# Loading q and k of the first two batches by token range, and moving block 1's attention work to later places

## The chip, the cores and the metric

The kernel runs on one core of a Trainium2 chip. A core has a matrix engine (TensorE, PE in the profile, with its weight loads as PEld), a vector engine (VectorE, DVE), an activation engine (ScalarE, ACT), a general engine (GpSimd, POOL) and a queue engine (SyncE, SP); sixteen DMA engines move data between device memory and the on-chip SBUF. Matrix products land in PSUM banks. Each engine works through its own list of instructions in order, and semaphores tie the lists together. The metric is the device time of one execution in microseconds (us).

## The reference

Eight batches of attention in chunks of 64 tokens are followed by a gated two-layer product over all 4608 tokens.

```python
# q, k, v: (8 batches, 8 heads, 576 tokens, 64), cut into 9 chunks of 64
scores = scale * q_c @ k_c.T            # per chunk, 64 x 64
attn = softmax(scores)
x = (attn @ v_c) -> (8*576 tokens, 8*64)
h = x @ w_in                            # 512 -> 2048
g = h * sigmoid(beta * h)
out = g @ w_out                         # 2048 -> 512, float32
```

## The kernel before, in words

The 4608 tokens are worked on in nine blocks of 512 (`BLK`). A batch has 576 tokens, so a block and a batch do not coincide: block 0 is tokens 0 to 511 of batch 0; block 1 is tokens 512 to 575 of batch 0 and 0 to 447 of batch 1. A group `g` of scores is four chunks (256 tokens), two groups to a block; a tile `i` of PV is 128 tokens, four to a block.

For one block the work is: scores (`emit_sc`, L156), exponentials on ScalarE (L178), the product with v and a column of ones (`emit_pv`, L212), division by the sum on VectorE (`normed`, L190 and L191), a transpose of the 128-token tile into `xt`, by TensorE and a ScalarE copy (`emit_xp`, L232, L238) or by a DMA transpose (L222), then L1 (16 products `m` with w_in, each followed by a Silu on ScalarE: `emit_h` L259, `emit_g` L270) and L2 (products with w_out). `emit_m(j, m, pieces)` writes one `m` of L1 in `pieces` column ranges. Block 0 has its own entrance: `head_sc`, `head_pv`, `head_xp` and `L1_first`, which work by halves of the heads (`z`) so that they can begin before all heads are there. Blocks from 1 on use a seven-product scheme (Strassen-Winograd) for L2 (`steps_L2`, with sums of `gt` by `emit_sum` and differences of w_out by `emit_tw`), blocks from 2 on also for part of L1. L2 of block 0 (`L2_plain(0)`) is plain: twenty units, for t = 0 to 3 in turn, over w_out rows 0-3, 4-7, 8-11, 12-13 and 14-15; the first twelve units hold four products each and the last eight two each. It holds all four PSUM banks of pool `ps_p`, one per t, and its result is copied by ScalarE (even t, L535) or VectorE (odd t, L533).

w_out is divided by beta row group by row group (`scale_w_out`): most on VectorE (L126), some on ScalarE (L122, the argument `act`). q and k arrive as [32 t-lines x 4 heads, run of tokens, 64] and are brought into [64 dims, tokens] form by 32x32 block transposes on VectorE (`emit_T`, L135), one for q and one for k per half of the heads.

Order is written by hand (`manual_schedule`): every engine does its instructions as the program lists them. All loads that convert float32 to float16 are issued by GpSimd into one queue: q and k of batch 0 (four loads), v of batch 0 (four), w_in (five), w_out 0-1 and 2-3 (a pair number covers 256 rows), q and k of batch 1 (four), w_out 4-5, v of batch 1 (four), w_out 6, w_out 7, q and k of batch 2, and so on. The eight load semaphores are used in turn, so GpSimd issues a load only after the one eight places ahead has landed. The buffers for raw q and k are two deep (`qk`), so batch 3 writes where batch 1 was; transposed q and k are three deep (`qt`); `ps_s` (tags sc0, sc1) and `ps_x` (tag x) hold one buffer each.

Inside `L2_plain(0)` the dictionary `hooks` puts block 1's attention between the units: scores of groups 2 and 3 ahead of unit 8, PV of tiles 4 to 7 ahead of units 11, 12, 14, 16, the tile transposes ahead of 12, 14, 16, 18, and the scalings of w_out rows 12 to 15 ahead of 11 and 14. `L1_plain(1, ...)` follows, with its own hooks for VectorE's later transposes and w_out differences.

Of the kernel before, what the change touches and what calls it, by code (L numbers as in the profile page):

```python
# [15 lines left out]
def kernel(  # L16
# [10 lines left out]
    nc = tc.nc  # L27
# [9 lines left out]
    BLK = 512  # L37
    NB = NT // BLK
    HM = DM // 2
    VP = 80  # L40
    scale = 1.0 / float(D) ** 0.5

# [38 lines left out]
    q_t = {}  # L81
    k_t = {}

    def load_qk(b, split=False):
        for dst, nm in ((q_t, "qu"), (k_t, "ku")):
            dst[b] = qk_p.tile([128, 2, RUN, D], FP16, tag=nm, name=nm)
        for zs in ((slice(0, 1), slice(1, 2)) if split else (slice(0, 2),)):
            for src, dst in ((q, q_t), (k, k_t)):
                nc.gpsimd.dma_start(
                    out=dst[b][:, zs].rearrange("p z r d -> p z (r d)"),  # L90
                    in_=src[b].rearrange("(z a) (t r) d -> (a t) z (r d)", z=2, r=RUN)[:, zs],
                )

    def load_v(b, zs=(0, 1)):
        t = vbuf[b % NV]
        for z in zs:
            for hp in range(2):
                h0 = 4 * z + 2 * hp
                nc.gpsimd.dma_start(  # L99
                    out=t[64 * hp:64 * hp + 64, 2 * z:2 * z + 2, :, 0:D].rearrange(  # L100
                        "p s c d -> p (s c) d"),
                    in_=v[b, h0:h0 + 2].rearrange("s (c p) d -> p (s c) d", p=CH),
                )
# [8 lines left out]
    def load_w_out(m0, n=2):  # L112
        nc.gpsimd.dma_start(
            out=w_out16[:, m0:m0 + n].rearrange("p m r d -> p m (r d)"),
            in_=moe_w_out[m0 * 256:(m0 + n) * 256, :].rearrange(
                "(m p r) d -> p m (r d)", p=128, r=2),
        )
# [10 lines left out]
    qT = {}  # L128
    kT = {}

    def emit_T(b, z, which):
        src, dst, nm = ((q_t, qT, "qT"), (k_t, kT, "kT"))[which]
        if b not in dst:
            dst[b] = qt_p.tile([128, 2, 32, RUN, 2], FP16, tag=nm, name=nm)
        nc.vector.transpose(  # L135
            out=dst[b][:, z].rearrange("p t r e -> p (t r e)").bitcast(FP32).rearrange(
                "p (t r) -> p r t", r=RUN),
            in_=src[b][:, z].rearrange("p r d -> p (r d)").bitcast(FP32).rearrange(
                "p (r d) -> p r d", r=RUN),
        )  # L140

    def T_items(b):
        return [lambda z=z, w=w: emit_T(b, z, w) for z in range(2) for w in range(2)]

    et_t = {}
    sc_h = {}
# [1 line left out]
    def sc_part(g, z, sc):  # L148
        for c in range(4):
            b, cb = divmod(4 * g + c, NCB)  # L150
            for e in range(2):
                for a in range(4):
                    p0, o0 = 32 * a, 64 * (a // 2)
                    kk = kT[b][p0:p0 + 32, z].rearrange("p t r e -> p (t r) e")
                    qq = qT[b][p0:p0 + 32, z].rearrange("p t r e -> p (t r) e")
                    nc.tensor.matmul(  # L156
                        out=sc[a % 2][o0:o0 + 64, z, c, :],
                        lhsT=kk[:, cb * CH:(cb + 1) * CH, e],
                        rhs=qq[:, cb * CH:(cb + 1) * CH, e],
                        start=(e == 0),  # L160
                        stop=(e == 1),
                    )
# [436 lines left out]
    def L1_first():  # L599
        gt_t[0] = gt_p.tile([128, KFF, BLK], FP16, tag="gt", name="gt")  # L600

        def part(g, z):
            for m in range(4):
                emit_h(0, m, g * 256, (g + 1) * 256, (z, 2 + z))
                if (g, z) == (1, 1):
                    emit_g(0, m)

        part(0, 0)
        head_xp(0, 1, "x")
        table(ACTF.Silu)  # L610
        part(1, 0)
        head_xp(1, 1, "s1", eng=nc.vector)
        part(0, 1)
        part(1, 1)
        for m in range(4, 6):
            hps_t[0, m] = ps_s.tile([128, BLK], FP32, tag=f"sc{m % 2}", name="hps")
        for m in range(4, KFF):
            emit_m(0, m, 4 if m < 12 else 1)

    def L1_plain(j, hooks, pieces={}):  # L620
        gt_t[j] = gt_p.tile([128, KFF, BLK], FP16, tag="gt", name="gt")
        for m in range(KFF):
            hooks.get(m, lambda: None)()
            emit_m(j, m, pieces.get(m, 1))
            if m == 8:
                for p in (0, 2):
                    emit_sum(j, 3, p)
        for p in range(4):
            fill.extend([lambda w=w, p=p: emit_sum(j, w, p) for w in (1, 2)])
        hooks.get(KFF, lambda: None)()  # L630
# [24 lines left out]
        nc.scalar.activation(out=warm2, in_=warm, func=func, scale=1.0)  # L655

    with tc.manual_schedule():
        load_qk(0, split=True)
        nc.vector.memset(zero, 0.0)
        nc.vector.memset(bstage, 0.0)  # L660
        nc.vector.memset(warm, 0.0)
# [13 lines left out]
            load_w_in(g)  # L675
        load_w_out(0)
        load_w_out(2)
        load_qk(1, split=True)
        load_w_out(4)
        load_v(1)  # L680
        load_w_out(6, 1)
        load_w_out(7, 1)
        load_qk(2)

        d = emit_idle(88, w=8)
        emit_idle(11, d=d)
        for f in T_items(0):
            f()
        nc.vector.transpose(
            out=bt, in_=bstage.rearrange("p r i -> p (r i)").rearrange("p (i r) -> p r i", r=2)  # L690
# [23 lines left out]
        emit_sw()  # L714
        scale_w_out(range(0, 4))
        scale_w_out(range(4, 8))
        for f in T_items(1):
            f()
        scale_w_out(range(8, 12), act=2)
        emit_tw(1)  # L720
        table(ACTF.Exp)
        load_v(2)
        load_qk(3)
        hooks = {
            8: lambda: [emit_sc(2, "x"), emit_sc(3)],
            11: lambda: [emit_pv(4, xbar=False), scale_w_out((12, 13), act=1)],
            12: lambda: [emit_pv(5, xbar=False), emit_xp(4)],
            14: lambda: [scale_w_out((14, 15), act=1), emit_pv(6, xbar=False), emit_xp(5)],
            16: lambda: [emit_pv(7, xbar=False), emit_xp(6)],
            18: lambda: [emit_xp(7), table(ACTF.Silu)],  # L730
        }
        for kk, f in enumerate(L2_plain(0)):
            hooks.get(kk, lambda: None)()
# [17 lines left out]
        for j in range(1, NB):  # L751
            na = j + 1
            late = j == 1
            if late:
                L1_plain(1, {
                    3: lambda: emit_tw(3), 4: lambda: T(2), 5: lambda: T(2),
                    6: lambda: emit_tw(2), 7: lambda: T(2), 9: lambda: T(2),
                    10: lambda: emit_tw(4), 14: lambda: T(3), 15: lambda: T(3),
                    11: lambda: [loads(1), loads_v(1)],
                    KFF: lambda: [table(ACTF.Exp), emit_sc(4, "x"), emit_sc(5)],  # L760
                }, pieces={0: 4, 1: 4, 2: 4, 3: 4, 4: 4, 5: 2})
            else:
                L1(j, {8: lambda: loads(j), 10: lambda: T(j + 2), 11: lambda: loads_v(j),
                       13: lambda: T(j + 2), 14: lambda: T(j + 2) if j + 2 < B else [dve(2), emit_sum(j, 3, 0)],
                       15: lambda: [dve(2), emit_sum(j, 3, 2)] if j + 2 >= B else None})

            def pv(n, where):
                if na < NB:
                    emit_pv(4 * na + n, where)

            mm, cB, cD, cC = steps_L2(j, last=(j == NB - 1))
            def pvs(n):
                pv(n, "x")
                pv(n + 1, "s")
# [74 lines left out]
```

The softmax here doesn't subtract the row's maximum and nothing guards it: scores larger than these inputs give would overflow.

## Time and profile before

| | |
|---|---|
| median of 3 executions | 276.07 us (276.04 to 276.81) |
| profiled execution, own time | 276.81 us |
| its span in the profile | 275.0 us |
| TensorE busy | 266.9 us (97%) |
| VectorE busy | 214.9 us (78%) |
| ScalarE busy | 164.3 us (60%) |
| GpSimd busy | 96.8 us (35%) |
| granted TensorE clock | full in all 40 slices |
| queue of converting loads (q0) | 18.35 MB, 45024 packets |
| queue of stores and DMA transposes (q1) | 12.99 MB, 24448 packets |

The profile is one execution. "Busy" adds up the time of an engine's instructions; the chain of work that ended last follows the execution back from its last instruction, at each step to what released it. In lists of instructions the columns are start, duration, engine, line, operation, output and input, and in brackets the time that the engine stood idle ahead of it and what ended the wait. The difference between an execution's own time and its span lies outside the engines' instructions. The ends of TensorE products are modelled, so two groups that follow each other closely can overlap in the list.

### The profile page before, as it was taken

What the parts mean: (1) busy time and instruction counts of PE and PEld (TensorE: products, weight loads), DVE (VectorE), ACT (ScalarE), POOL (GpSimd) and SP (SyncE); (2) the same over time, 40 slices, a digit from 0 to 9 for tenths busy, and PEclk for the clock granted to TensorE, in tenths of its full rate; (3) what the DMA queues carried; (4) which work ended last, traced back from release to release, by engine and by line L of the source; (5) the groups of instructions that cost most, each with busy time, mean ns of one, the idle gap of its engine ahead of it and who ended that gap; (6) DMA issues with size and microseconds to landing.
All of it is one profiled execution on the core that took longest, in us unless ns stands there. A gap on an engine that the chain in (4) does not pass through costs nothing.

```text
span 275.0 us, 8686 instructions
## 1 busy us (share of the span) xinstructions
PE 266.9 (97%) x3751; PEld 197.1 (72%) x3751; DVE 214.9 (78%) x429; ACT 164.3 (60%) x281; POOL 96.8 (35%) x107
## 2 busy tenths in 40 slices
PE   8699999999999999999999999999999999999994
PEld 5379544857886688768876886688668866886784
DVE  2673674877888999799989988997689768986844
ACT  2169527879166845784578447854784478316820
POOL 8643446171108720772077205720311031112110
PEclk9999999999999999999999999999999999999999
DMA  6999999999967934893479242924202320232013
GB/s 103 171 200 210 210 181 208 194 261 199 90 135 144 172 44 117 173 163 42 117 158 173 45 120 76 87 42 117 79 0 60 100 76 0 55 104 76 0 42 114
DMA packets 69654, 32.02 MB, mean 116 GB/s; under 512 B 53744, under 2 KB 63984, under 8 KB 69616
## 3 DMA queue, kind: packets, MB, share of 16 engines
q0 software_dynamic: 45024, 18.35, 55.3%
q1 hardware_dynamic: 24448, 12.99, 18.1%
q8 instruction: 29, 0.48, 0.7%
q10 hardware_dynamic: 144, 0.13, 0.1%
q14 instruction: 9, 0.07, 0.1%
HBM read 36.71 MB, written 9.44 MB: 168 GB/s over the span
## 4 chain that ended last, share of the span: by engine, by line
PE 79%; DMA 14%; DVE 3%; issue 1%; ACT 1%; POOL 1%; DVEq 0%; ACTq 0%; POOLq 0%
PE hps L259 22%; PE oA L416 19%; PE wA L313 9%; PE wX L313 7%; DMA w_out<-in_moe_w_out_dram 6%; PE oB L416 5%; PE oD L416 5%; DMA wi<-in_moe_w_in_dram 4%; PE oC L416 4%; DMA ku<-in_k_dram 3%; PE ops L518 2%; PE x L212 2%; DMA xt<-x 1%; PE scx L156 1%; PE sc L156 1%
## 5 line engine op out<-in xcount | busy, mean ns | idle before, releaser
L259 PE MATMUL hps<-xt,wi 128*128 128x512 f16 (+2 forms) x528 | 85.2, 308 | 0.2
L270 ACT ACTIVATE gt<-hps,beta 128x512 f16<-128x512 f32 x88 | 57.8, 683 | 20.9 <-PE hps L259 20.7
L259 PEld LDWEIGHTS <-wi 128*128 128x128 f16 x528 | 42.8, 98 | 23.2 <-DMA wi<-in_moe_w_in_dram 0.2
L416 PEld LDWEIGHTS <-s 128*128 128x128 f16 x496 | 47.6, 98 | 6.2 <-DVE s L376 0.5
L416 PE MATMUL oA<-tw,s 128*128 128x256 f16 x368 | 44.2, 273 | 0.0
L416 PEld LDWEIGHTS <-gt 128*128 128x128 f16 x384 | 36.3, 98 | 6.6
L427 ACT COPY u<-oA 128x512 f32<-128x512 f32 x24 | 14.0, 585 | 40.3 <-PE oA L416 40.3
L321 DVE COPY u<-wA 128x512 f32<-128x512 f32 x42 | 28.6, 682 | 4.5 <-PE wA L313 4.5
L99 POOL DMA_DIRECT2D vb<-in_v_dram x32 | 27.4, 873 | 6.3 <-DMA w_out<-in_moe_w_out_dram 3.3
L344 POOL TENSOR_TENSOR t<-u,w 128x512 f32<-128x512 f32 x14 | 17.8, 1274 | 33.5 <-DVE u L321 33.5
L313 PEld LDWEIGHTS <-sw 128*128 128x128 f16 x224 | 21.9, 98 | 9.2 <-issue 0.7
L486 POOL TENSOR_TENSOR o<-t,o 128x512 f32<-128x512 f32 x7 | 8.9, 1271 | 51.7 <-ACT o L483 42.9
L454 POOL TENSOR_TENSOR w<-u,u 128x512 f32<-128x512 f32 x7 | 9.8, 1407 | 47.2 <-ACT u L427 25.9
L135 DVE STREAM_TRANSPOSE qT<-qu 128x576 f32<-128x576 f32 x16 | 20.0, 1252 | 6.4 <-DMA qu<-in_q_dram 6.2
L135 DVE STREAM_TRANSPOSE kT<-ku 128x576 f32<-128x576 f32 x16 | 19.9, 1244 | 3.6 <-DMA ku<-in_k_dram 3.5
L313 PEld LDWEIGHTS <-wi 128*128 128x128 f16 x168 | 16.4, 98 | 4.9
L655 ACT ACT_TABLE_LOAD x15 | 19.2, 1283 | 0.3
L324 ACT ACTIVATE gt<-c,beta 128x512 f16<-128x512 f32 x28 | 18.7, 716 | 0.3
L374 DVE TENSOR_TENSOR s<-gt 128x512 f16<-128x512 f16 x32 | 17.8, 555 | 0.0
L313 PE MATMUL wA<-xs,sw 128*128 128x256 f16 x112 | 16.8, 273 | 0.5 <-DVE u L321 0.5
L376 DVE TENSOR_TENSOR s<-s,gt 128x512 f16<-128x512 f16 x32 | 15.6, 488 | 1.1
L518 PE MATMUL ops<-w_out,gt 128*128 128x512 f16 x64 | 15.1, 379 | 0.4 <-ACT w_out L122 0.2
(96 smaller groups left out, 404.6 us busy)
## 6 DMA issues: line engine op xcount, KB each, us to landing
out_dram<-osb SPq DMA_DIRECT2D x21, 256.0 KB, 3.1
vb<-in_v_dram POOLq DMA_DIRECT2D x32, 144.0 KB, 8.1
out_dram<-o SPq DMA_DIRECT2D x14, 256.0 KB, 2.2
qu<-in_q_dram POOLq DMA_DIRECT2D x6, 576.0 KB, 7.8
ku<-in_k_dram POOLq DMA_DIRECT2D x6, 576.0 KB, 10.0
wi<-in_moe_w_in_dram POOLq DMA_DIRECT2D x3, 512.0 KB, 11.5
w_out<-in_moe_w_out_dram POOLq DMA_DIRECT2D x3, 512.0 KB, 15.5
qu<-in_q_dram POOLq DMA_DIRECT2D x4, 288.0 KB, 12.0
```

The source lines that it names most:

```text
L99: nc.gpsimd.dma_start(out=t[64 * hp:64 * hp + 64, 2 * z:2 * z + 2, :, 0:D].rearrange("p s c d -> p (s c) d"), in_=v[b, h0:h0 + 2].rearrang ...
L135: nc.vector.transpose(out=dst[b][:, z].rearrange("p t r e -> p (t r e)").bitcast(FP32).rearrange("p (t r) -> p r t", r=RUN), in_=src[b][:, ...
L259: nc.tensor.matmul(out=hps_t[j, m][:, c0:c1], lhsT=w_r[m // 4][:, 2 * z + e, m // 2 % 2, m % 2, :], rhs=xt_t[j][:, n, c0:c1], start=(n == ...
L270: nc.scalar.activation(out=gt_t[j][:, m, :], in_=hps, func=ACTF.Silu, scale=beta2[:, m % 2, m // 2:m // 2 + 1],)
L313: nc.tensor.matmul(out=bank[b][:, i, :], lhsT=a[:, kk, q, i, :], rhs=rhs[:, kk, :], start=(first and i == 0 and kk == 0), stop=(kk == 1), ...
L321: nc.vector.tensor_copy(out=sb[nm], in_=bank[b])
L324: nc.scalar.activation(out=gt_t[j][:, m, cols], in_=src, func=ACTF.Silu, scale=beta2[:, m % 2, m // 2:m // 2 + 1],)
L344: nc.gpsimd.tensor_tensor(out=sb["t"], in0=sb["u3"], in1=sb["w1"], op=ALU.add)
L374: tt(out=s1[:, lo], in0=g[:, lo, dn], in1=g[:, hi, dn], op=ALU.add)
L416: nc.tensor.matmul(out=bank[name][:, i, :], lhsT=a[:, kk, i * 128:(i + 1) * 128], rhs=b[:, kk, :], start=(first and i == 0 and n == 0), st ...
L518: nc.tensor.matmul(out=ops[t], lhsT=gt_t[j][:, kk, t * 128:(t + 1) * 128], rhs=wo(kk), start=(kk == 0), stop=(kk == KFF - 1),)
L655: nc.scalar.activation(out=warm2, in_=warm, func=func, scale=1.0)
```

## The change

Batches 0 and 1 are loaded and transposed by token range. `S0` is 512: batch 0's tokens 0 to 511 are loaded first (four loads), tokens 512 to 575 only after w_out 2-3 (four loads more). `S1` is 448: batch 1's tokens 0 to 447 come after w_out 4-5, which moves ahead of them, and tokens 448 to 575 after w_out 7. w_out 6 moves ahead of batch 1's v. A partial load gives each of the 32 t-lines its own shorter run of tokens, 16, 2, 14 or 4 in place of 18. The transposes are split in the same way, and the tile that they write is declared by token (`S`) instead of by line and run.

Block 1's attention moves: scores of groups 2 and 3 ahead of unit 10, PV of tiles 4 to 7 ahead of units 13, 14, 16, 19, with tile 5 in pool `ps_s`; tile transposes ahead of 17, 18, 19, and that of tile 7 into `L1_plain`. The scalings of rows 12 to 15 stand ahead of units 12 and 15. `L1_plain` begins with its first four `m` by token tiles of 128, and their four Silus follow together. In block 0, m 10 and 11 of L1 are written in one piece instead of four; in block 1 the pieces are 4, 4, 4, 2 for m 4 to 7.

```diff
+    S0, S1 = BLK, 2 * BLK - S
...
-    def load_qk(b, split=False):
-        for dst, nm in ((q_t, "qu"), (k_t, "ku")):
-            dst[b] = qk_p.tile([128, 2, RUN, D], FP16, tag=nm, name=nm)
-        for zs in ((slice(0, 1), slice(1, 2)) if split else (slice(0, 2),)):
+    def load_qk(b, t0=0, t1=S):
+        r0, r1 = t0 // 32, t1 // 32
+        if t0 == 0:
+            for dst, nm in ((q_t, "qu"), (k_t, "ku")):
+                dst[b] = qk_p.tile([128, 2, RUN, D], FP16, tag=nm, name=nm)
+        if (t0, t1) == (0, S):
...
+            return
+        for z in range(2):
+            for src, dst in ((q, q_t), (k, k_t)):
+                nc.gpsimd.dma_start(
+                    out=dst[b][:, z, r0:r1].rearrange("p r d -> p (r d)"),
+                    in_=src[b, 4 * z:4 * z + 4, t0:t1].rearrange(
+                        "a (t r) d -> a t (r d)", r=r1 - r0),
                 )
...
-    def emit_T(b, z, which):
+    def emit_T(b, z, which, t0=0, t1=S):
         src, dst, nm = ((q_t, qT, "qT"), (k_t, kT, "kT"))[which]
+        r0, r1 = t0 // 32, t1 // 32
         if b not in dst:
-            dst[b] = qt_p.tile([128, 2, 32, RUN, 2], FP16, tag=nm, name=nm)
+            dst[b] = qt_p.tile([128, 2, S, 2], FP16, tag=nm, name=nm)
         nc.vector.transpose(
-            out=dst[b][:, z].rearrange("p t r e -> p (t r e)").bitcast(FP32).rearrange(
-                "p (t r) -> p r t", r=RUN),
-            in_=src[b][:, z].rearrange("p r d -> p (r d)").bitcast(FP32).rearrange(
-                "p (r d) -> p r d", r=RUN),
+            out=dst[b][:, z, t0:t1].rearrange("p s e -> p (s e)").bitcast(FP32).rearrange(
+                "p (t r) -> p r t", r=r1 - r0),
+            in_=src[b][:, z, r0:r1].rearrange("p r d -> p (r d)").bitcast(FP32).rearrange(
+                "p (r d) -> p r d", r=r1 - r0),
         )
...
-            emit_m(0, m, 4 if m < 12 else 1)
+            emit_m(0, m, 4 if m < 10 else 1)
...
-        for m in range(KFF):
+        for t in range(4):
+            if t == 2:
+                emit_xp(7)
+            for m in range(4):
+                emit_h(j, m, t * 128, (t + 1) * 128)
+        for m in range(4):
+            emit_g(j, m)
+        for m in range(4, KFF):
...
-        load_qk(0, split=True)
+        load_qk(0, 0, S0)
...
-        load_qk(1, split=True)
+        load_qk(0, S0, S)
         load_w_out(4)
+        load_qk(1, 0, S1)
+        load_w_out(6, 1)
         load_v(1)
-        load_w_out(6, 1)
         load_w_out(7, 1)
+        load_qk(1, S1, S)
         load_qk(2)
...
-        for f in T_items(0):
+        for f in T_items(0, 0, S0):
...
-        for f in T_items(1):
+        for f in T_items(0, S0, S):
             f()
+        emit_tw(1)
         scale_w_out(range(8, 12), act=2)
-        emit_tw(1)
+        for f in T_items(1, 0, S1):
+            f()
...
-            8: lambda: [emit_sc(2, "x"), emit_sc(3)],
-            11: lambda: [emit_pv(4, xbar=False), scale_w_out((12, 13), act=1)],
-            12: lambda: [emit_pv(5, xbar=False), emit_xp(4)],
-            14: lambda: [scale_w_out((14, 15), act=1), emit_pv(6, xbar=False), emit_xp(5)],
-            16: lambda: [emit_pv(7, xbar=False), emit_xp(6)],
-            18: lambda: [emit_xp(7), table(ACTF.Silu)],
+            10: lambda: [emit_sc(2, "x"), emit_sc(3)],
+            12: lambda: scale_w_out((12, 13), act=1),
+            13: lambda: emit_pv(4, xbar=False),
+            14: lambda: emit_pv(5, "s", xbar=False),
+            15: lambda: scale_w_out((14, 15), act=1),
+            16: lambda: emit_pv(6, xbar=False),
+            17: lambda: emit_xp(4),
+            18: lambda: emit_xp(5),
+            19: lambda: [emit_pv(7, xbar=False), emit_xp(6), table(ACTF.Silu)],
...
-                    3: lambda: emit_tw(3), 4: lambda: T(2), 5: lambda: T(2),
-                    6: lambda: emit_tw(2), 7: lambda: T(2), 9: lambda: T(2),
+                    4: lambda: [emit_tw(3), [f() for f in T_items(1, S1, S)], T(2)],
+                    5: lambda: T(2), 6: lambda: emit_tw(2), 7: lambda: T(2), 9: lambda: T(2),
...
-                }, pieces={0: 4, 1: 4, 2: 4, 3: 4, 4: 4, 5: 2})
+                }, pieces={4: 4, 5: 4, 6: 4, 7: 2})
```

More of the change, by code (lines that the diff above doesn't have):

```diff
@@ L82 @@
     k_t = {}
-    def load_qk(b, split=False):
-        for dst, nm in ((q_t, "qu"), (k_t, "ku")):
-            dst[b] = qk_p.tile([128, 2, RUN, D], FP16, tag=nm, name=nm)
-        for zs in ((slice(0, 1), slice(1, 2)) if split else (slice(0, 2),)):
+    def load_qk(b, t0=0, t1=S):
[4 more added lines that the diff above has]
+        if (t0, t1) == (0, S):
             for src, dst in ((q, q_t), (k, k_t)):
                 nc.gpsimd.dma_start(
-                    out=dst[b][:, zs].rearrange("p z r d -> p z (r d)"),
-                    in_=src[b].rearrange("(z a) (t r) d -> (a t) z (r d)", z=2, r=RUN)[:, zs],
+                    out=dst[b].rearrange("p z r d -> p z (r d)"),
+                    in_=src[b].rearrange("(z a) (t r) d -> (a t) z (r d)", z=2, r=RUN),
+                )
+            return
[5 more added lines that the diff above has]
+                        "a (t r) d -> a t (r d)", r=r1 - r0),
                 )
@@ L129, with T_items @@
     kT = {}
-    def emit_T(b, z, which):
+    def emit_T(b, z, which, t0=0, t1=S):
         src, dst, nm = ((q_t, qT, "qT"), (k_t, kT, "kT"))[which]
+        r0, r1 = t0 // 32, t1 // 32
         if b not in dst:
-            dst[b] = qt_p.tile([128, 2, 32, RUN, 2], FP16, tag=nm, name=nm)
+            dst[b] = qt_p.tile([128, 2, S, 2], FP16, tag=nm, name=nm)
         nc.vector.transpose(
-            out=dst[b][:, z].rearrange("p t r e -> p (t r e)").bitcast(FP32).rearrange(
-                "p (t r) -> p r t", r=RUN),
-            in_=src[b][:, z].rearrange("p r d -> p (r d)").bitcast(FP32).rearrange(
-                "p (r d) -> p r d", r=RUN),
-        )
-    def T_items(b):
-        return [lambda z=z, w=w: emit_T(b, z, w) for z in range(2) for w in range(2)]
+            out=dst[b][:, z, t0:t1].rearrange("p s e -> p (s e)").bitcast(FP32).rearrange(
+                "p (t r) -> p r t", r=r1 - r0),
+            in_=src[b][:, z, r0:r1].rearrange("p r d -> p (r d)").bitcast(FP32).rearrange(
+                "p (r d) -> p r d", r=r1 - r0),
+        )
+    def T_items(b, *ts):
+        return [lambda z=z, w=w: emit_T(b, z, w, *ts) for z in range(2) for w in range(2)]
     et_t = {}
@@ L153, in sc_part @@
                     p0, o0 = 32 * a, 64 * (a // 2)
-                    kk = kT[b][p0:p0 + 32, z].rearrange("p t r e -> p (t r) e")
-                    qq = qT[b][p0:p0 + 32, z].rearrange("p t r e -> p (t r) e")
+                    kk = kT[b][p0:p0 + 32, z]
+                    qq = qT[b][p0:p0 + 32, z]
                     nc.tensor.matmul(
```

## The prediction

> **What bounds the kernel now.** I read the page's busy table first, then the chain of waits, then the timeline of the first 85 us, because every edit lies before 66 us.
>
> ```profile
> PE 266.9 (97%) x3751; PEld 197.1 (72%) x3751; DVE 214.9 (78%) x429; ACT 164.3 (60%) x281; POOL 96.8 (35%) x107
> ...
> PE 79%; DMA 14%; DVE 3%; issue 1%; ACT 1%; POOL 1%; DVEq 0%; ACTq 0%; POOLq 0%
> ```
>
> TensorE is the bound; the other 14% is the load queue at the start. The chain in order of time names its pieces:
>
> ```profile
> 3.03 8.74 DMA ku<-in_k_dram
> 12.05 11.51 DMA wi<-in_moe_w_in_dram
> 23.84 15.47 DMA w_out<-in_moe_w_out_dram
> 39.39 1.34 ACT w_out L122 x2
> 40.77 2.53 PE ops L518 x11
> ```
>
> The first useful work waits for k of batch 0; block 0's second product then waits for w_out rows 8 to 11, queued behind all of q and k of batch 1. From the timeline, the gates that the change moves:
>
> ```profile
> 11.79 1.26 DVE L135 STREAM_TRANSPOSE kT<-ku 128x576 f32<-128x576 f32 x1 [0.34 <-DMA ku<-in_k_dram]
> 13.10 0.45 PE L156 MATMUL sc<-qT,kT 32*64 32x64 f16 x32 [1.92 <-DVE bt L689]
> 17.22 0.77 PEld L259 LDWEIGHTS <-wi 128*128 128x128 f16 x8 [0.25 <-DMA wi<-in_moe_w_in_dram]
> 31.77 7.07 PE L518 MATMUL ops<-w_out,gt 128*128 128x512 f16 x32
> 50.39 0.69 DVE L533 COPY osb<-ops 128x512 f32<-128x512 f32 x1 [0.42 <-PE ops L518]
> 63.38 1.26 DVE L135 STREAM_TRANSPOSE kT<-ku 128x576 f32<-128x576 f32 x1 [2.44 <-DMA ku<-in_k_dram]
> 73.58 0.21 DVE L190 RECIPROCAL rd<-x 128x8 f32<-128x8 f32 x1 [1.08 <-PE x L212]
> ```
>
> The bracket is the engine's idle time ahead of the line and who ended it. From 17.22 to 268 us TensorE hardly stops: a gain must come from a start before 17.22 or from gaps inside 38.7 to 54 us.
>
> The trace's completion records (a load has landed with its sixteenth completion) give: k of batch 0 at 7.44 and 11.77, first w_in half 17.18, w_out 2-3 at 31.08, last k of batch 1 at 36.69, w_out 4-5 at 39.31, last v of batch 1 at 43.49, w_out 6 and 7 at 44.23 and 45.48, last v of batch 2 at 55.59, k of batch 3 at 63.36. GpSimd issues each load some 0.29 us after the one eight places ahead has landed, so the queue is always full and acts as one server.
>
> **What the Trainium skill says.** "DMA: Bandwidth & Descriptors", Bandwidth, gives 0.95 us for one 64 KB load issued by GpSimd and calls transfers under 64 KB descriptor-dominated. No load of this trace has that size; queued v loads (144 KB, 128-byte packets) follow each other by about 1.05 us. "Perfetto Trace Analysis", Tensor Engine Instruction, calls ScalarE and VectorE strict FIFO; the trace agrees: L122 idled 6.7 us while nothing passed it. "ScalarE: Activation LUTs", What ACT_TABLE_LOAD costs, gives 1283 ns for a table load, as here (1283), and a further 1380 ns drain, which does not show here: the load of 40.74 is followed at 42.03.
>
> **The change part by part.**
>
> Head. Each of the four q, k loads of batch 0 has 2048-byte instead of 2304-byte packets. Queued loads show 1.40 us for 2304 (q of batch 1: 32.47, 33.87, 35.26) and 1.25 for 2048 (w_out, 2.50 per two), so 8 packets per engine take 0.155 instead of 0.175 us each. Over 32 packets that is 0.64 us. Bounds: 0 (packet count unchanged, and the start may be limited by it) and 0.97 (a ninth of 8.74). I take 0.64. The last transpose, 16/18 of 1.26, is 0.14 shorter, but w_in's landing then decides: 16.54. First product 0.64 earlier. In block 0, m 10 and 11 in one piece take 0.86 instead of 0.89: 0.06. L2(0) starts at 31.77 - 0.70 = 31.07.
>
> Queue. Remainders: 256-byte packets (batch 0) and 512-byte (batch 1), 8 per engine and load. Between 128 bytes (13.4 ns per packet from 1191 per us) and 1024 (79 ns from 203 per us) the line gives 23 and 42 ns: 0.18 and 0.33 us per load. So batch 0's rest costs 0.8 us, w_out 4-5 lands at 30.44 + 0.8 + 2.6 = 33.9, and four first parts of batch 1 (1.10 each, 14/18) at 38.3. Last v of batch 1: the queue has carried w_out 6 (+1.25) and lacks 2/9 of q and k (-1.24), with the small packets 43.8. Eight more issues of 0.55 us lie on GpSimd, which has room.
>
> L2(0). Forty matmuls at 0.219 (7.0 us for 32) end at 39.82. Batch 0's rest and the table (1.22) are over by 34; w_out 8-11 scaled by 35.3: the old wait is gone, with 4 us of cover. The last of four 0.98 us transposes ends at 39.3, 0.5 before the scores need it. Scores 1.32, units 10, 11 1.73: TensorE at unit 12 is at +3.05. ScalarE, in order: exp of the scores from +0.77 to +2.77 (as 103.91 to 104.68, 1.02 and 1.08), then row 12's scaling 0.72, ready at +3.45: **stall 0.4**. PV of tile 4 at 43.7, about when v lands (0.1). From PV 4's start TensorE needs PV 0.25, unit 13 0.43, PV 5 0.25, units 14, 15 0.87, PV 6 0.25 and row 14's product 0.22 to reach row 15: 2.27. VectorE starts norm 4 0.38 after PV (46.28 to 46.66), takes 0.93, norm 5 in its split form 1.20 (15.31 to 16.49), row 15's scaling 0.35 and 0.04 to be seen: 2.90, **stall 0.63**. Behind the scaling wait norm 6 and PV 7; these have cover. TensorE leaves L2(0) at about 49.25.
>
> L1(1). Its first four m now need all four PSUM banks of L2(0) at once. ops 3 is copied by VectorE behind norm 7, which starts 0.54 before L2(0) ends: 0.9 + 0.69 + 0.06 gives 1.11 after the end, the fourth m arrives at 0.66: **stall 0.45**. Then four silus end together and m 4 waits for the first bank: **0.18**. Tile 7's transposes (0.24) only move from L2(0) into L1(1); ScalarE's copy behind the table load is ready before its quarter. Before, m 4 started at 54.0 (silu 3 at 54.14), 22.23 after 31.77. Pure work there is 14.0 (64 products of L2) + 1.33 (scores) + 1.0 (four PV) + 0.96 (four tile transposes) + 3.57 (four m of 0.893, silus 54.14 and 55.03) = 20.86, so 1.37 us was waiting. After, stalls are 0.4 + 0.1 + 0.63 + 0.45 + 0.18, about 1.75: m 4 at 31.07 + 20.86 + 1.75 = 53.7. The added pieces (4, 4, 4, 2 for m 4 to 7 against 4, 2, 1, 1) cost 0.06. Sum: -0.70 + 0.38 + 0.06, about **-0.25**.
>
> Small terms. The transposes now write with strides of 16, 14, 4 and 2 elements instead of 18, which this trace lacks; from the rows I take no difference (0.1 us each way per transpose: batch 1's four sit in the shadow of their loads, only the last shows). Twelve more short ones take 4 x 0.21 and 4 x 0.34, on VectorE while TensorE multiplies, less 4 x 0.14 and 4 x 0.28 saved on the long ones. Block 0's output copies come about 1.5 us earlier, so their stores share the DMA engines with v of batch 2 instead of q and k of batch 3; the megabyte is moved before k of batch 3 either way, so its landing stays put. SP's queue has the same orders.
>
> Behind it. q of batch 3 overwrites batch 1's buffer, so GpSimd now waits for batch 1's rest: copy of ops 3 to 50.4, table 1.22, four transposes of 0.34 (0.21 for 64 columns, 2.03 ns per further column): 53.0. Behind this wait stand k of batch 3, GpSimd's s3 sums and the next loads. v of batch 2 occupies the DMA engines to 56.0, and the first packets of the kernel moved about 1.3 us after their issue, so 1.4 us of cover remains. k of batch 3 lands about 0.5 later; VectorE, in order, is late by 0.5 with sums, norms and block 2's transposes. Cover: the 1.08 us at 73.58, less the PSUM release before PV at 73.20, leaves 0.7. Cost 0; past it one for one. The rest of the program has the same order.
>
> The sum is against the profiled execution, 276.81 (span 275.0, 1.8 outside): 276.56. That execution was the longest of three; from their median, 276.07, the forecast is 275.8.
>
> **Rivals.** *Clean L2(0)*: scaling and bank copies arrive in time (0.63 and 0.45 vanish): 274.7. For it: VectorE is 78% busy and I stacked separate latencies. Against: the three waits follow from queue order. *No head gain*: start limited by packet count, not bytes; 276.4. For it: only 60 to 77 packets per us moved from 3 to 6 us against 88 to 94 later. *Slower, short loads*: the page's 0.95 us is the span of a lone 64 KB load; in a full queue part of it overlaps. If half of the excess stays, each of batch 0's four remainders holds the queue 0.57 instead of 0.18, everything behind lands 1.5 later: last k of batch 1 at 39.8, its transpose ends at 40.8, the scores wait 1.0, and the last v, 45.3, holds PV 4 (44.7) by 0.5 more: 277.3. With all of it, 278.8. It decides once the four take over 1.3 us together (0.8 and the 0.5 of slack before the scores). Against it: 1152 packets of a v load take only 1.05, and 128 are here to be moved.
>
> **How the numbers follow.** Forecast 0.48 (own range 275.3 to 276.4), clean 0.22, no head gain 0.12, short loads 0.18. A measurement here can tell about 0.3%, 0.83 us. Faster (under 275.24): most of clean and a tenth of the forecast, 0.24. Slower (over 276.9): most of short loads and small tails, 0.20. Same 0.56. The range 274.6 to 277.4 holds the forecast, no head gain (bound 276.4; the other bound of the head, 0.97, gives 275.5), most of clean and half of short loads.
>
> **What would show it.** Right: first w_in product near 16.6; w_out 4-5 no longer on the chain; ScalarE's row 12 and VectorE's row 15 named as what TensorE waits for in 43 to 47; a VectorE wait at L1(1)'s fourth m; k of batch 3 0.5 later without TensorE idle at 73 to 75. Wrong: a head gain outside 0 to 1; scores waiting for k of batch 1; a gap of over 0.5 near 80 us; any difference after 85 us beyond the shift.

## The result and the profile after

The changed kernel is slower: 284.38 us median of four executions (283.26 to 285.75) against 276.22 (276.04 to 276.81) for the kernel before, a ratio of 1.029 (95% interval 1.024 to 1.035). The forecast was 275.8 with a range up to 277.4, so it missed by 8.6 us and on the wrong side. The traced execution took 283.63 us (span 281.8) against 276.81 (span 275.0): it holds 6.8 of the 8.2 us, and the readings below are of it.

Busy time by engine, and the shares of the chain that ended last, from the page of the changed kernel:

```profile
PE 268.6 (95%) x3751; PEld 197.6 (70%) x3751; DVE 213.9 (76%) x439; ACT 163.9 (58%) x281; POOL 103.6 (37%) x115
...
PE 66%; DMA 21%; DVE 6%; issue 3%; POOL 2%; ACT 0%; DVEq 0%; POOLq 0%; ACTq 0%
```

TensorE has the same 3751 products and 1.7 us more busy time; DMA's share of the chain rose from 14% to 21%. The pieces of that chain (start, duration, what) show the loads in a row up to 48 us, with gaps of 0.3 to 1.9 us, and one more at 58:

```profile
2.14 10.40 DMA ku<-in_k_dram
14.44 11.24 DMA wi<-in_moe_w_in_dram
25.97 11.28 DMA w_out<-in_moe_w_out_dram
37.55 10.11 DMA vb<-in_v_dram
...
58.29 12.29 DMA ku<-in_k_dram
```

The timeline of the changed kernel at the places that the prediction named:

```profile
10.26 1.03 DVE L147 STREAM_TRANSPOSE qT<-qu 128x512 f32<-128x512 f32 x1 [8.57 <-DMA qu<-in_q_dram]
...
13.66 0.64 PE L168 MATMUL sc<-qT,kT 32*64 32x64 f16 x32 [5.61 <-DVE kT L147]
...
14.66 3.17 PE L256 MATMUL idle<-zero 128*128 128x512 f16 x7
...
17.76 0.45 PE L168 MATMUL sc<-qT,kT 32*64 32x64 f16 x32
...
21.68 1.05 PE L271 MATMUL hps<-xt,wi 128*128 128x256 f16 x8
...
70.61 1.26 DVE L147 STREAM_TRANSPOSE kT<-ku 128x576 f32<-128x576 f32 x1 [1.53 <-DMA ku<-in_k_dram]
...
78.67 0.32 PE L224 MATMUL x<-vb,et 64*64 64x65 f16 x16 [0.48 <-DVE x L203]
```

VectorE's first transpose waits 8.57 us for q of batch 0, and TensorE 5.61 us for the transposed k. Starts of the same events in the two traces, in us:

| event | before | after | later by | grew here by |
|---|---|---|---|---|
| first scores | 8.77 | 13.66 | 4.89 | 4.89 |
| first w_in product | 17.22 | 21.68 | 4.46 | -0.43 |
| L2(0) | 31.77 | 36.17 | 4.40 | -0.06 |
| L1(1) | 50.19 | 54.37 | 4.18 | -0.22 |
| scores of block 2 | 64.43 | 69.35 | 4.92 | 0.74 |
| L1(2) | 80.44 | 86.74 | 6.30 | 1.38 |
| span | 275.0 | 281.8 | 6.8 | 0.5 |

The loss is made before the first w_in product and after 54 us. L2(0), where most of the edits lie, is 0.2 shorter than before. In the head the first scores come 4.89 later. From them to the second scores, through the seven dummies, TensorE works 4.10 us where before it worked 2.41. In return the wait of 1.92 ahead of the second scores, which the prediction's lines show at 13.10, is gone, and the rest up to the first w_in product is 0.20 shorter: 4.89 + 1.69 - 1.92 - 0.20 makes the 4.46.

Why the first load is late stands in the completion records. One load has sixteen; here are those of batch 0's loads, in us (load 1 is q of the first half of the heads, load 2 its k, loads 3 and 4 the second half):

```
before, load 1:  sixteen from 4.80 to 5.66
after, load 1:   3.39 3.40 3.40 3.41 3.42 3.45 3.49 3.53 3.54 3.56 3.56 3.57 | 9.92 10.16 10.18 10.24
after, load 2:   eight from 4.09 to 4.22 | eight from 10.46 to 12.54
after, load 3:   4.74 4.79 4.82 4.84 | twelve from 10.88 to 13.05
after, load 4:   none early | sixteen from 11.20 to 14.16
```

Before, sixteen completions fall within 0.9 us. After, twelve come at once, as from DMA engines with nothing to move, and four come 6.4 us later. Of the loads behind it eight, four and none come early, which is what is left free if each load takes four other engines. The four loads land at 10.24, 12.54, 13.05 and 14.16 instead of 5.66, 7.43, 10.16 and 11.76. The Trainium skill has this in "DMA: Bandwidth & Descriptors", section "Why a DMA increments its semaphore by 16 and not by 1": a load runs on as many engines, up to 16, as divide the size of the outermost dimension of both its patterns, and all sixteen report for a load that GpSimd issues, whatever its shape. The source of a whole batch is 128 rows at one distance, 18 lines of 64 values. A token range cut out of every head leaves 4 heads at one distance and 32 rows at another; they no longer form one row of 128, the outermost dimension of the source is 4, and the records fit four engines.

What this does to the first 16 us is in the DMA view of each kernel: 40 slices of 0.4 us, busy share of the sixteen engines in tenths, then GB/s. First the changed kernel:

```profile
DMA  0000000913382497966979799999999999999999
GB/s 0 0 0 0 0 5 6 32 3 33 44 78 36 82 82 102 99 109 82 123 113 159 143 205 175 151 195 198 163 179 170 149 167 166 152 169 164 170 173 177
DMA packets 6274, 1.70 MB, mean 106 GB/s; under 512 B 5645, under 2 KB 5761, under 8 KB 6273
```

and the kernel of the first experiment below, which has the same loads with rows that lie at one distance:

```profile
DMA  0000004679999998999999999999999999999999
GB/s 0 0 0 0 0 5 52 94 129 161 175 172 188 186 159 143 221 174 184 179 174 159 179 144 144 151 155 156 153 157 152 163 168 189 155 172 192 212 202 200
DMA packets 5905, 2.24 MB, mean 140 GB/s; under 512 B 4829, under 2 KB 5392, under 8 KB 5904
```

Up to 8 us (twenty slices times 0.4 us) the changed kernel moves 0.37 MB, the other 0.89; from 8 to 16 us both move 1.3. The 0.52 MB that are missing are 3.0 us of queue at the 174 GB/s of 8.35 to 17.22 us in the second kernel. The engines fill slowly, which fits in part loads handed out one after another of which each occupies four.

### The profile page after: what moved, and what is told of

It is laid out like the page before. It is cut to its first block, busy times and chain, and to the rows that moved or that the text cites. A ratio compares the mean times of both kernels' runs of the same rounds, so it can differ in the third digit from the quotient of the medians.

```text
span 281.8 us, 8704 instructions
## 1 busy us (share of the span) xinstructions
PE 268.6 (95%) x3751; PEld 197.6 (70%) x3751; DVE 213.9 (76%) x439; ACT 163.9 (58%) x281; POOL 103.6 (37%) x115
## 4 chain that ended last, share of the span: by engine, by line
PE 66%; DMA 21%; DVE 6%; issue 3%; POOL 2%; ACT 0%; DVEq 0%; POOLq 0%; ACTq 0%
PE oA L428 17%; PE hps L271 17%; PE wA L325 9%; DMA ku<-in_k_dram 8%; PE wX L325 6%; PE oB L428 5%; PE oD L428 4%; DMA w_out<-in_moe_w_out_dram 4%; DMA wi<-in_moe_w_in_dram 4%; PE oC L428 4%; DMA vb<-in_v_dram 4%; DMA xt<-x 1%; PE sc L168 1%; PE scx L168 1%; PE x L224 1%
## 5 line engine op out<-in xcount | busy, mean ns | idle before, releaser
L147 DVE STREAM_TRANSPOSE qT<-qu 128x576 f32<-128x576 f32 (+4 forms) x20 | 20.2, 1009 | 14.9 <-DMA qu<-in_q_dram 14.9
L147 DVE STREAM_TRANSPOSE kT<-ku 128x576 f32<-128x576 f32 (+4 forms) x20 | 20.0, 1001 | 3.0 <-DMA ku<-in_k_dram 3.0
L168 PEld LDWEIGHTS <-kT 32*64 32x64 f16 x1152 | 11.3, 107 | 9.3 <-DVE kT L147 6.2
```

The source lines that it names most:

```text
L147: nc.vector.transpose(out=dst[b][:, z, t0:t1].rearrange("p s e -> p (s e)").bitcast(FP32).rearrange("p (t r) -> p r t", r=r1 - r0), in_=sr ...
L168: nc.tensor.matmul(out=sc[a % 2][o0:o0 + 64, z, c, :], lhsT=kk[:, cb * CH:(cb + 1) * CH, e], rhs=qq[:, cb * CH:(cb + 1) * CH, e], start=(e ...
```

## The experiments

**The same loads, rows at one distance.** Rival: the smaller packets or the doubled number of loads themselves cost the time. This kernel, and the two below that are built on it, read other tokens for batches 0 and 1 (16 or 14 lines of each row of 18), so the bytes, rows, loads and order are those of the change, but the source is 128 rows at one distance.

```diff
-    in_=src[b, 4 * z:4 * z + 4, t0:t1].rearrange(
-        "a (t r) d -> a t (r d)", r=r1 - r0),
+    in_=src[b].rearrange("(z a) (t r) d -> (a t) z (r d)", z=2, r=RUN)[
+        :, z, r0 * D:r1 * D],
```

> The changed kernel, with the source of every partial load taken as 128 rows of equal distance (tokens 18t to 18t+15, and so on, of each head) in place of 4 heads x 32 rows. Sizes, packets, counts and orders are those of the changed kernel; only which tokens are loaded is different, so the scores belong to other tokens and the output is not the reference's. Theory (a load whose source begins with a dimension of 4 is put on 4 of the 16 DMA engines): q and k of batch 0 land by 11.5 us in place of 14.1, the first score begins near 8.5 in place of 13.7, block 0's second product near 31.5 in place of 36.2, k of batch 1's first part lands near 39, and the time is 275.5 to 277.5. Rival 1 (shorter rows and more loads cost the queue more, whatever the engines): nothing of this, 283 to 285. Rival 2 (the wait of batch 3's loads for batch 1's rest and the new order in L1(1) cost most of it): the head is regained and 279 to 281 remain.

Measured: 277.22 us, ratio 1.0031 (1.0010 to 1.0052), in the expected range; traced 277.07 with a span of 275.3. Of the 2.9% only 0.3% is left: about 7.3 of 8.2 us are regained. The sixteen completions of the first load fall between 4.52 and 5.36, and the four loads end at 10.48. Its timeline:

```profile
8.35 0.53 PE L168 MATMUL sc<-qT,kT 32*64 32x64 f16 x32
...
10.51 1.03 DVE L147 STREAM_TRANSPOSE kT<-ku 128x512 f32<-128x512 f32 x1 [0.34 <-DMA ku<-in_k_dram]
...
15.77 1.05 PE L271 MATMUL hps<-xt,wi 128*128 128x256 f16 x8 [0.19 <-DMA wi<-in_moe_w_in_dram]
...
42.42 0.59 PE L530 MATMUL ops<-w_out,gt 128*128 128x512 f16 x2 [0.33 <-ACT w_out L133]
...
46.07 0.38 PE L530 MATMUL ops<-w_out,gt 128*128 128x512 f16 x1 [0.35 <-DVE w_out L137]
...
49.64 1.28 PE L271 MATMUL hps<-xt,wi 128*128 128x128 f16 x20 [0.21 <-DVE osb L545]
...
64.34 1.26 DVE L147 STREAM_TRANSPOSE kT<-ku 128x576 f32<-128x576 f32 x1 [1.52 <-DMA ku<-in_k_dram]
...
73.51 0.32 PE L224 MATMUL xp<-vb,et 64*64 64x65 f16 x15 [0.34 <-DVE x L203]
...
80.48 0.60 PE L325 MATMUL wA<-xt,wi 128*128 128x256 f16 x4
```

Three waits of the prediction's L2(0) and L1(1) steps are here, by line and releaser: row 12, row 15 and the fourth m. Those of 0.1 at PV of tile 4 and 0.18 at m 4 do not show in the list.

The pages of the two kernels show the split of the loads once more, in the line of the load queue (packets, MB, share of sixteen engines). The changed kernel:

```profile
q0 software_dynamic: 52320, 18.38, 58.1%
```

and this one:

```profile
q0 software_dynamic: 46176, 18.35, 55.9%
```

The changed kernel has 6144 packets more for nearly the same bytes. In the packet records they are all 4 bytes long. For sixteen partial loads that is 384 each, or 32 for each of twelve engines, as many as each of the other four has rows to carry. The pattern of the source is the cause; the size and number of the rows are not.

**One batch at a time.** First only batch 0 by token range, batch 1 whole and block 1 in its old places (on the kernel before):

```diff
-        load_qk(0, split=True)
+        load_qk(0, 0, S0)
...
-        load_qk(1, split=True)
+        load_qk(0, S0, S)
+        load_qk(1)
```

> The kernel before, with batch 0 alone split by token range (first parts first, rest after w_out 2-3, transposes split); batch 1, hooks and L1 of block 1 as before. Theory: the whole head loss of 4.4 us (first w_in product at 21.7 in place of 17.2), but the old wait for w_out 4-5 inside L2(0) (0.85 us) is covered by the delay: 279.5 to 280.5. Rival 2 (head is not where it is lost): 276 to 277.5.

Measured, in one execution: 281.62 us, span 279.9, above the expected 279.5 to 280.5. L2(0) starts 4.94 later than before, and lasts 17.68 us until L1(1) instead of 18.42: old waits inside it are covered by the late start. The changed kernel's late head gives batch 1's loads the same time.

Then only batch 1 by token range, with all of the new order and places (on the changed kernel):

```diff
-        load_qk(0, 0, S0)
+        load_qk(0)
...
-        load_qk(0, S0, S)
```

> The changed kernel with batch 0 loaded and transposed whole, as before; batch 1 stays split (four engines a load), hooks and L1 of block 1 as in the changed kernel. Theory: head as before (first w_in product near 17.2), then q and k of batch 1 take some 6.5 us in the queue in place of 4.4, the scores of block 1 wait 0.6, L1(1) loses 0.7, k of batch 3 lands some 3.5 late and costs a further 1.6: 278 to 279.5. Rival (batch 0's split is all of it): 275.5 to 276.5.

Measured: 279.00 us, ratio 1.0099 (1.0061 to 1.0138), in the expected range. The four loads of batch 1 land within 0.7 us of each other, at 39.14, 39.41, 39.61 and 39.82, so that their four transposes, one engine's work, follow in a row. The timeline of this kernel:

```profile
39.17 0.95 DVE L155 STREAM_TRANSPOSE qT<-qu 128x448 f32<-128x448 f32 x1 [4.17 <-DMA qu<-in_q_dram]
...
41.51 0.91 DVE L155 STREAM_TRANSPOSE kT<-ku 128x448 f32<-128x448 f32 x1
...
42.48 0.38 PE L176 MATMUL scx<-qT,kT 32*64 32x64 f16 x24 [1.09 <-DVE kT L155]
```

TensorE waits 1.09 for the last of them. With landings 1.1 apart, as in the first experiment, only the last transpose would have been in the way. L2(0) becomes 19.65 long (18.42 before). Losses of 5.3 and 2.7 us of the two parts make 8.0, against 8.2 for both; the first is a single execution.

**Order and places alone.** Rival to all of this: the new order of loads and the new places in L2(0) and L1(1) have a cost of their own. Both batches are loaded whole:

```diff
-        load_qk(0, 0, S0)
+        load_qk(0)
...
-        load_qk(0, S0, S)
         load_w_out(4)
-        load_qk(1, 0, S1)
+        load_qk(1)
...
-        load_qk(1, S1, S)
```

> The changed kernel with batches 0 and 1 both loaded and transposed whole, on sixteen engines: what remains of the change is the order of the loads (w_out 4-5 ahead of batch 1, w_out 6 ahead of its v) and the new places of block 1's attention. Theory: head as before (first w_in product 17.2); k of batch 1 lands at 39.3, its last transpose ends at 40.6 when the scores come at 40.5, stalls in L2(0) and L1(1) about 1.7 where the kernel before had 1.4: 276.0 to 277.0 where before is 276.2. Rival (the new places are a loss of their own): over 277.5.

Measured: 276.94 us, ratio 1.0003 (0.9988 to 1.0019), as expected. Order and places are neutral: the whole loss of the change comes with the partial loads.

The reverse, in which the partial loads with rows at one distance keep the order but block 1 goes back to its old places and L1(1) begins as before:

```diff
-            10: lambda: [emit_sc(2, "x"), emit_sc(3)],
...
+            8: lambda: [emit_sc(2, "x"), emit_sc(3)],
+            11: lambda: [emit_pv(4, xbar=False), scale_w_out((12, 13), act=1)],
...
```

> e1 (other tokens in batches 0 and 1) with block 1's scores, PV and tile transposes at the places of the kernel before, and L1 of block 1 in its old order; only loads, transposes and block 0's pieces are the changed ones. Theory: the new places cost 0.75 us in L1(1) (a PSUM bank and a copy behind a table load), and save about as much in L2(0), where the old places would wait about 1.1 for batch 1's k and 1 for its v: block 2's scores within 0.4 of e1's 63.6, and the time within 0.6 of e1. Rival (the new places are what keeps e1 from gaining): 276.4 or less.

Measured: 278.85 us, ratio 1.0057 (1.0036 to 1.0077). That is more than 0.6 us above the first experiment, against expectation, though the intervals of the two ratios overlap. In its timeline the scores wait for k of batch 1:

```profile
40.20 0.38 PE L168 MATMUL scx<-qT,kT 32*64 32x64 f16 x24 [1.81 <-DVE kT L147]
```

Scores of block 2 start at 65.01 instead of 63.59; 0.61 of this is a later head, about 0.8 comes behind it. But that k lands at 39.18 here, 1.79 later than in the first experiment with the same loads in the same order: fifteen of its completions are there by 37.18, and one engine trails. With the landings of the first experiment this wait would be about gone, so it is not shown that the later places are needed when w_out 4-5 goes ahead of batch 1.

**TensorE's clock in the head.** The page gives the changed kernel a granted clock of 0.7 in its second and third slices, 7 to 21 us. Stretches of 2 us of it (PE, PEld, DVE, ACT and POOL busy, then the granted clock, DMA share, GB/s):

```profile
8.00:10.00 2.00, 0.05 (x1) 0.00 (x0) 0.00 (x0) 0.00 (x0) 0.16 (x1) 1.00 0.95 159
10.00:12.00 2.00, 0.00 (x0) 0.00 (x0) 1.03 (x1) 0.00 (x0) 0.73 (x1) 0.74 1.46 177
12.00:14.00 2.00, 0.34 (x25) 0.34 (x28) 1.43 (x2) 0.00 (x0) 1.17 (x2) 0.50 1.99 161
14.00:16.00 2.00, 2.00 (x60) 1.11 (x50) 1.90 (x6) 1.21 (x4) 1.47 (x3) 0.50 2.11 171
16.00:18.00 2.00, 2.00 (x33) 0.61 (x35) 0.34 (x2) 0.00 (x0) 1.04 (x2) 0.55 1.60 192
```

TensorE stands idle from 8.05 to 13.66 and then runs at half clock, so the seven dummy products behind the first scores take 3.17 us where they took 1.69. In the Trainium skill "TensorE: Matmul & The Clock Gate", Part 1, says that the clock falls to half after an idle window of about 3.4 us. The trace agrees that it falls after idling, but its clock records put the fall at 10.97, after 2.9 us. Rival to a late queue: the clock is what costs the time. 24 dummies ahead of the first scores instead of 11, then 37:

```diff
-        emit_idle(11, d=d)
+        emit_idle(24, d=d)
```

> The changed kernel with 13 more dummy products of 512 columns ahead of the first scores, so that TensorE does not idle from 8 to 13.7 us. Theory of the head: 2.3 us of its 4.46 us are the late loads and the rest is the seven dummies behind the first scores, 3.2 us long in place of 1.7 at a granted clock of 0.6: with a full clock the second scores begin near 16.3 in place of 17.8 and the first w_in product near 20.3. Since the queue is late as well (first part of batch 1's k lands at 43.7), the scores of block 1 then wait and the end moves by 0 to 0.8 us only: 283 to 284.4. Rival (the clock is all that costs in the head): end earlier by 1.4 or more, under 283.

Measured: 283.83 us, ratio 1.0274 (1.0230 to 1.0318). The time is in the expected range, but not by its theory: the first w_in product starts at 21.58 and not at 20.3. The dummies ended at 11.0, and the clock fell all the same:

```profile
14.00:16.00 2.00, 2.00 (x68) 1.03 (x61) 1.93 (x5) 1.21 (x4) 1.51 (x3) 0.68 2.29 163
16.00:18.00 2.00, 2.00 (x44) 0.86 (x46) 0.49 (x3) 0.00 (x0) 1.17 (x2) 0.50 1.66 189
```

With 37:

> The changed kernel with 26 more dummy products of 512 columns ahead of the first scores (e3 had 13, which ended at 11 us, and the clock still fell in 14 to 18). They now reach to 13.7. Theory: the granted clock stays full, the seven dummies behind the first scores take 1.7 in place of 3.2 us and the first w_in product comes at 20.2 in place of 21.7; then block 1's scores wait for its k, which lands near 43.6 with a transpose of 0.95 behind it, and the end moves by under 0.8 us: 283 to 284.4. Rival (the head's delay goes straight to the end): 282.9 or less.

Measured: 284.52 us, ratio 1.0265 (1.0245 to 1.0286), 0.1 above the expected range. Its clock is full in these two stretches, and its timeline has the dummies at full speed:

```profile
15.31 1.68 PE L256 MATMUL idle<-zero 128*128 128x512 f16 x7
...
20.84 1.05 PE L271 MATMUL hps<-xt,wi 128*128 128x256 f16 x8
...
23.09 0.81 PE L271 MATMUL hps<-xt,wi 128*128 128x256 f16 x6 [0.76 <-issue]
...
45.58 0.82 PEld L168 LDWEIGHTS <-kT 32*64 32x64 f16 x88 [0.21 <-DVE kT L147]
```

The first w_in product comes 0.84 earlier than in the changed kernel, yet L1(0) then takes 15.41 us instead of 14.49, and L2(0) starts at 36.25 instead of 36.17. Most of this is a pause of 0.76 for which the profile names no releaser; its cause is open. The gain would have been lost later all the same: even so the second half of block 1's scores waits 0.21 for its transposed k. In the changed kernel this half starts at 45.28, just as its transposed k is ready (45.23). A faster head has nothing to win there: the queue is the bound.

**Sixteen engines for the reference's tokens.** Loads of 32 rows, one per head, have an outermost dimension of 32. Batch 0's first part is sixteen such loads; batch 1 is whole, and q and k of batch 3 are issued ahead of v of batch 2.

```diff
+                    for a in range(4):
+                        nc.gpsimd.dma_start(
+                            out=dst[b][32 * a:32 * a + 32, z, r0:r1].rearrange("p r d -> p (r d)"),
+                            in_=src[b, 4 * z + a, t0:t1].rearrange("(t r) d -> t (r d)", r=r1 - r0),
+                        )
```

> A version with the reference's tokens: the changed kernel with batch 0's first parts loaded head by head (sixteen loads of 32 rows, which are to spread over all sixteen engines), batch 1 loaded and transposed whole behind w_out 4-5, and q and k of batch 3 ahead of v of batch 2. Theory: issue on GpSimd (some 0.5 us each) holds the sixteen loads only a little; k of batch 0 lands near 11, first w_in product near 16.5, block 1's scores wait up to 0.8 for its k; 275 to 276.5. Rival (sixteen issues at 0.6 us delay v and w_in): first w_in product after 18, 277 to 279.

Measured: 281.30 us, ratio 1.0149 (1.0119 to 1.0180), above the expected range and above the rival's. The loads do spread (the first one's completions all fall between 3.66 and 3.90), although they read the very rows that the changed kernel reads, so the rows' addresses are not the cause. But GpSimd's own time to issue them now holds w_in back; its issues in the timeline, and the first product:

```profile
1.27 2.17 POOL L109 DMA_DIRECT2D qu<-in_q_dram  x4 [0.82 <-POOLq L875]
...
14.06 3.67 POOL L135 DMA_DIRECT2D wi<-in_moe_w_in_dram  x5
...
19.98 1.05 PE L288 MATMUL hps<-xt,wi 128*128 128x256 f16 x8 [1.10 <-DMA wi<-in_moe_w_in_dram]
```

Four loads of 32 rows take 2.17 us to issue, 0.54 each, about as much as a load of 128 rows in the kernel before (0.55), and sixteen of them stand ahead of w_in. Later k of batch 1, landing at 44.16, makes the scores wait another 1.79.

**k of batch 3.** In the first experiment's kernel L1(2) starts at 80.48 although the scores of block 2 are 0.84 ahead of the kernel before. q and k of batch 3 moved ahead of v of batch 2, on that kernel:

```diff
-        load_v(2)
         load_qk(3)
+        load_v(2)
```

> e1 (sixteen engines a load; other tokens than the reference's in batches 0 and 1) with one edit more: q and k of batch 3 are issued ahead of v of batch 2. In e1 the head gains 1.45 us, block 2's scores are still 0.84 early, but L1(2) begins 0.04 late: k of batch 3 lands at 64.25 while TensorE comes earlier. Theory (VectorE, waiting in order for k of batch 3, takes the gain back): k of batch 3 lands near 61, block 2's PV no longer waits for a PSUM release, L1(2) begins near 79.5 and the time falls by 0.7 to 1.2 us against e1, to 276.0 to 276.5 where e1 was 277.2. Rival (the loss in 64 to 80 us has another cause, the wait of batch 3's loads for batch 1's rest, which stays and now holds v of batch 2 as well): same as e1 or slower.

Measured: 277.05 us, ratio 1.0013 (0.9988 to 1.0037), above the expected 276.0 to 276.5. k lands at 61.26 instead of 64.32, PV no longer waits, and L1(2) starts 1.2 earlier; from its timeline:

```profile
61.28 1.26 DVE L147 STREAM_TRANSPOSE kT<-ku 128x576 f32<-128x576 f32 x1 [1.14 <-DMA ku<-in_k_dram]
...
71.98 0.32 PE L224 MATMUL x<-vb,et 64*64 64x65 f16 x16
...
79.27 0.60 PE L325 MATMUL wA<-xt,wi 128*128 128x256 f16 x4
```

The traced execution, 275.64, is the shortest of the twenty; the ratio is 0.2% better than in the first experiment and the intervals overlap, so a gain in time is not shown. The same swap on the kernel before:

> The kernel before with one edit: q and k of batch 3 issued ahead of v of batch 2. In e5 this edit moved L1(2) from 80.5 to 79.3. Theory: VectorE no longer waits 2.44 us for k of batch 3 at 63; v of batch 2 lands by 64, before its PV at 69.2; TensorE's 0.5 us gap at 80 closes: L1(2) at 79.9 and 0.3 to 0.6 us less, 275.5 where before is 276.0. Rival (the gap at 80 is the transposing DMA's own time, whatever VectorE did before): no change.

Measured: 276.41 us, ratio 1.0001 (0.9983 to 1.0020): no change, as its rival said. From scores of block 2 to L1(2) it takes 16.03 us (16.01 before), although k of batch 3 lands 5 us earlier: in the kernel before it is hidden, in keeping with the prediction's cover of 0.7. No kernel of the study was measurably faster than the kernel before.

## Why the prediction was wrong

**Head** failed, and with it the forecast. "Each of the four q, k loads of batch 0 has 2048-byte instead of 2304-byte packets ... so 8 packets per engine": the packets are as much shorter as was taken (median 0.173 us in the trace, against 0.192 for 2304 bytes), but a load has 32 of them on each of four engines, not 8 on each of sixteen. That a shortened load still spreads over all sixteen was assumed without a reason. Instead of 0.70 earlier, L2(0) came 4.40 later. With sixteen engines the step holds in sign: the first w_in product started at 15.77, 15.71 and 16.38 in three kernels with short rows against 17.22, 17.29, 17.55 and 16.56 in four with whole ones, 1.2 earlier on average instead of 0.64. The groups spread over 0.7 and 1.0 us, so the size stays open. In part the spread is one engine that trails: at the last k of batch 0 its completion comes 1.05 behind the fifteenth in the kernel before and 0.45 in the first experiment.

**Queue** failed on the same assumption. Batch 0's rest took 1.64 us instead of 0.8, and the four first parts of batch 1 6.5 instead of 4.4. With rows at one distance they took 0.79 and 4.40, the last v of batch 1 landed at 43.09 (43.8 predicted).

**L2(0) and L1(1)** held in their main places, once the loads ran on sixteen engines. Row 12 stalled 0.33 (0.4), row 15 0.35 (0.63). The fourth m came 0.37 late (0.45 predicted: it started at 49.64, 1.04 after L1(1) began at 48.60, with 0.67 of work between); its bracket shows 0.21 of this. The stretch from L2(0) to L1(1) took 18.33 (18.18), the one from there to block 2's scores 14.99 against 14.24 before, where 0.69 of stalls and pieces had been counted. Together the new places cost 0.66 us in this trace and 0.47 with whole loads, where 0.44 was forecast; the time of the kernel with whole loads shows no loss.

**Small terms** held where the runs can show it. In the changed kernel block 0's stores fall on v of batch 2, whose packets move at a sixth to a third of their rate beside them (last section), and the last v lands at 65.45 instead of 55.59. But "the megabyte is moved before k of batch 3 either way": this k lands at 70.58 instead of 63.36, 7.2 later, and k of batch 2, ahead of the stores, was already 7.0 late.

**Behind it** had the mechanism and mis-sized its first term. k of batch 3 was put 0.5 later and 0.7 covered. In the first experiment it lands 0.96 later while TensorE arrives 0.84 sooner, 1.80 in all; less 0.7, the cost "past it one for one" is 1.10, and 0.88 was measured between scores and L1(2). In the changed kernel k is 7.2 later and TensorE 4.9 later, which leaves 2.3, or 1.6 past the cover; 1.38 was lost.

Of the rivals, *Slower, short loads* pointed to the right place and the wrong mechanism: it priced the four rests at 0.57 each (0.41 measured) and took the head, where 4.5 us went, for safe. *No head gain* gave the head no loss as its worst. No rival asked on how many engines a load runs. Of its signs of a wrong prediction "a head gain outside 0 to 1" came true. "Scores waiting for k of batch 1" did not in the changed kernel, where L2(0) itself came late enough; it shows with the head regained (1.09 us with only batch 1 split).

Left open: from 6 to 8 us the changed kernel moves only 50 packets of 2048 bytes per us, though all four loads had been issued by 4.2 us (79 and 89 in the first experiment); the executions of the changed kernel outside the trace took up to 2.1 us more; and the 0.5 us lost behind 87 us have no cause found, though the stretch behind L1(2) differs by up to 1.4 us among the traces of this study. While batch 1's four loads take their 6.5 us, the queue does not stand still: packets of v, which is queued behind them, move from 39 us on, so engines that are done with a load go on to the next.

## What to carry to other kernels

Before a load is cut, write its source pattern down with the outermost dimension that is left: if its size is 4, a quarter of the DMA engines carry it. A range cut out of each of many runs can break the merge of two dimensions even though every packet stays long, and the fault shows in the completion records as a few late completions behind many early ones. A load queue is priced by what lands when, not by bytes alone: loads that run side by side land together, and the serial work that used to fit between them bunches up.

## What the runs showed of the hardware

The cheap cure for few engines, more loads, is bounded by GpSimd: 0.54 us of issue for each load of 32 rows. A load on four engines gives the other twelve work too: 32 packets of 4 bytes each, as the count of 6144 has it, and their completions come early. With 24 dummies the clock of TensorE fell at 14.71, by the clock records, after an idle stretch of only 2.8 us (11.0 to 13.8), shorter than the skill's window of 3.4, and 0.9 us after work had begun again. That the window runs free of the work, as the same section has it, can explain the delay; how much idle time is enough no run here isolates. The stretches at half clock in the head last 3.41 us here and 6.83 us in the changed kernel, once and twice that window. Stores and short-packet loads share the engines badly: with 101 to 149 store packets of 2048 bytes per us in 57 to 60 us of the changed kernel, v of batch 2 got 177 to 406 packets of 128 bytes per us; v of batch 1 got 1179 in 44 to 45 us, with no stores.
